# Loads of keys and queries around the block sums, transposes a batch ahead: a block-sparse attention with a gated feed-forward

## The chip, the cores and the metric

One core of a Trainium2 chip. The metric is the device time of one execution in microseconds (us), lower is better. A run counts as slow when it is over 1.5% above the fastest run of the same kernel; comparisons use fast runs only. With one core there is no second die to compare with, so this label rests on the time alone. In the profiles PE is TensorE's matmuls and PEld its weight loads, DVE is VectorE, ACT ScalarE, POOL GpSimd, and SP (its queue: SPq) SyncE. The granted clock is the TensorE clock that the throttle granted, 1.00 at full speed.

## The reference, cut to what matters

```python
# q, k, v: (4 batches, 8 heads, 768 positions, 64), float32
k_sum = k.reshape(B, H, 24, 32, D).max(axis=3)      # peak key of each block of 32
v_sum = v.reshape(B, H, 24, 32, D).mean(axis=3)     # mean value of each block
scores_l = scale * q @ k^T, only where |i - j| < 16
scores_s = scale * q @ k_sum^T + log(32)
a = softmax(concat([scores_l, scores_s]))
attn = a @ concat([v, v_sum])
x = attn.transpose(0, 2, 1, 3).reshape(3072, 512)
out = (sigmoid(x @ w_gate) * (x @ w_val)) @ w_out   # 512 -> 1536 -> 512
```

## The kernel before

The feed-forward network (FFN) of batch b is the base stream: 24 units of gate and value matmuls (`m1`, line L506) and 12 half-units of output matmuls for each half of the batch (`m2`). The attention steps of batch b+1 are dropped between these units by a slot number. So a step that waits holds up its engine, and with it the FFN behind it.

```python
def load_nat(b):                       # keys and queries of a batch, 16 casting DMAs
    ...
    for h in range(H):
        for nat, tap in ((kn, k), (qn, q)):
            nc.gpsimd.dma_start(out=nat[:, h // 2, :, ...], in_=tap[b, h]...)

def load_values(b):                    # one DMA for the whole batch
    load_v(b, 0, NU + 1) ...

# Attention steps
def D(self, p):                        # two transposing DMAs of a head pair, on SyncE's queue
    nc.sync.dma_start_transpose(kTn <- keys);  nc.sync.dma_start_transpose(qT <- queries)
def K(self, p): ...                    # DVE: peak keys (L254), then spread into kTx (L260, L262)
def L(self, g): ...                    # DMA: value rows by block, into vm
def R(self, g): ...                    # GpSimd: block sums of vm by halving additions (L417)
def M(self, g): ...                    # GpSimd: cast (L430), then a small DMA into vx
def B(self, g): ...                    # DVE: copies of the means inside vx (L435)
def H(self, g): ...                    # DVE: copies of neighbour rows inside vx, the halo (L365)
def A(self, p): ...                    # PE: probabilities times vx (L452), then DVE
def Y(self, p): ...                    # transposing DMA of the result into xT, on SyncE's queue
# T, Z, X: transposes and scores on PE; they play no part below

# end of the program's first part
load_values(1)
for g in range(2):
    a1.R(g)
...
NEXT = """
    3 T0   4 T1   5 Z0   6 T2   7 Z1   8 T3 M0 M1   10 Z2   12 Z3   13 H0 H1   15 B0 B1
    17 A0 A1   18 A2 A3 X0   19 X1   20 X2   21 X3"""
LATER = """
    0 R0 M0 R1 M1   2 K0   4 K1 D2   6 Z0 D3   8 K2 H0   10 Z1 H1   12 K3 B0   14 Z2 B1
    18 Z3   24 A0 A1   25 Y0   26 Y1   27 A2 A3   28 Y2   29 Y3"""
at[8].append(lambda: loads(2))
at.setdefault(14, []).append(lambda: block_rows(2))
at[23] = att[2].units("D0 D1")
```

GpSimd's queue is in order. It holds the casting loads and the block sums R, one behind the other, and this is where the change works.

The softmax here doesn't subtract the row's maximum and nothing guards it: scores larger than these inputs give would overflow.

Of the kernel before, what the change touches and what calls it, by code (L numbers as in the profile page):

```python
# [16 lines left out]
def kernel(  # L17
# [10 lines left out]
    nc = tc.nc  # L28

    B, H, S, D = q.shape  # L30
# [6 lines left out]
    NP = H // 2  # L37
    NU = H * NQ
# [21 lines left out]
    def ps(shape, dtype, name):  # L60
        return psum.tile(shape, dtype, name=name, tag="mm")

    def view(ap, off, dims):
        return bass.AP(ap.tensor, ap.offset + off, [list(ap.ap[0])] + [list(d) for d in dims])

    def rows_of(ap, off, dims):
        return bass.AP(ap.tensor, ap.offset + off, [list(d) for d in dims])
# [21 lines left out]
    def clear_ones(i):  # L89
        nc.vector.memset(vx_t[i][0:W, :, 64:66], 1.0)  # L90
        nc.vector.memset(vx_t[i][W:128, :, 64:66], 32.0)
# [29 lines left out]
    def make_zband():  # L121

        nc.vector.memset(zband, 0.0)
        with nc.allow_low_precision("zeros and ones"):
            nc.vector.tensor_reduce(out=zband[:, 29:32], in_=view(identp[0:W], 0, [[32, 3], [1, 32]]),
                                    axis=AX.X, op=ALU.add)
# [9 lines left out]
    def big():  # L136
        return vm_pool.tile([128, 2048], FP32, name="vm", tag="vm")

    def small():
        return nat_pool.tile([128, 3072], BF16, name="nat", tag="nat")  # L140

    def load_rows(tap, b, h0, nh, s0, n, st, queue=None):

        T = n // 128
        (queue or nc.gpsimd).dma_start(
            out=st.rearrange("p h t d -> p h (t d)"),
            in_=tap[b, h0:h0 + nh, s0:s0 + n, :].rearrange("h (p t) d -> p h (t d)", t=T))

    def load_nat(b):

        kn = small().rearrange("p (a c d) -> p a c d", a=NP, c=6)
        qn = small().rearrange("p (a c d) -> p a c d", a=NP, c=6)
        for h in range(H):
            for nat, tap in ((kn, k), (qn, q)):
                nc.gpsimd.dma_start(  # L155
                    out=nat[:, h // 2, :, 64 * (h % 2):64 * (h % 2) + 64],
                    in_=tap[b, h].rearrange("(c p) d -> p c d", p=128))
        return kn, qn

    def load_v(b, u0, u1, r0=0, r1=64):  # L160

        nc.gpsimd.dma_start(  # L162
            out=vx_t[b % 2][r0:r1, u0:u1, 0:64],
            in_=rows_of(v[b, 0, 0:1], (QT * u0 - 16 + r0) * D, [[D, r1 - r0], [QT * D, u1 - u0], [1, D]]))

    def load_values(b):
        if b + 1 < B:
            load_v(b, 0, NU + 1)
        else:
            load_v(b, 0, NU)  # L170
            load_v(b, NU, NU + 1, 0, 16)

    wg_bf = const.tile([128, NP, d_ff], BF16, name="wg")
# [365 lines left out]
    def run(base, at):  # L539
        for i, u in enumerate(base):  # L540
            u()
            for x in at.get(i, ()):
                x()

    def slots(text, a):
        at, slot = {}, None
        for w in text.split():
            if w.isdigit():
                slot = int(w)
            else:  # L550
                at.setdefault(slot, []).extend(a.units(w))
        return at
# [3 lines left out]
    att = [Attention(b, xTs[b]) for b in range(B)]  # L556


    a0 = att[0]

    k0 = [bf_pool.tile([128, 2, 6, 64], BF16, name="k0", tag="k0") for _ in range(NP)]
    qraw = small().bitcast(FP32).rearrange("p (h t d) -> p h t d", h=H, t=3)
    q0 = small().rearrange("p (a h t d) -> p a h t d", a=2, h=H, t=3)
    a0.ks = lambda p: k0[p]
    a0.qs = lambda p: q0[:, 0, 2 * p:2 * p + 2]
    a0.q2 = q0[:, 1]
    load_rows(q, 0, 0, 4, 0, HALF, qraw[:, 0:4], nc.sync)
    load_rows(q, 0, 4, 4, 0, HALF, qraw[:, 4:8], nc.sync)
    load_rows(k, 0, 0, 2, 0, S, k0[0])
    load_rows(k, 0, 2, 2, 0, S, k0[1])  # L570
    make_ident()
    load_rows(k, 0, 4, 2, 0, S, k0[2])
# [29 lines left out]
    load_wo(8, 4)  # L602

    nc.scalar.memzero(a0.heads(0, H, 0, 6, vx_t[0][96:128, 0:NU, 0:64]))
    f0 = Ffn(0, xTs[0])
    idle = ps([128, 512], FP32, "idle")
    a0.warm(idle[:, 0:128], 36)
    for i in range(2):
        clear_keys(i)
    make_masks()  # L610
# [1 line left out]
    for i in range(2, 4):  # L612
        clear_keys(i)
    a0.T1(0)
    a0.warm(idle[:, 0:128], 4)
    a0.T2(0, "dve")
    a0.S1(0, 0)
    a0.T1(1)
    a0.T2(1, "dve")
    a0.S1(0, 1)  # L620
    make_zband()
    a0.T1(2)
    a0.S1(1, 0, 4)
    a0.S1(1, 1)
    a0.T2(2, "dve")
    a0.T1(3)
    a0.S1(2, 0, 4)
    a0.S1(2, 1)
    a0.T2(3, "act")
    a0.S1(3, 0, 4)  # L630
    a0.halo(0, 2, 0, 6)
    a0.sums(0)
    a0.S1(3, 1)
    last = psum2.tile([128, 2, 512], FP32, name="last", tag="at")

    def wait(n):
        a0.warm(last[:, 0, 0:128], n)

    a0.means(0)
    a0.near(0)  # L640
    a0.halo(2, 4, 0, 6)
    a0.sums(1)
    a0.means(1)
    a0.far(0)
    a0.near(1)
    wait(4)
    a0.X(0, 0)
    a0.far(1)
    a0.halo(4, 6, 0, 6)
    a0.sums(2)  # L650
    a0.means(2)
    wait(4)
    a0.near(2)
    a0.X(1, 0)
    a0.far(2)
    a0.halo(6, 8, 0, 6)
    a0.sums(3)
    a0.means(3)
    wait(4)
    a0.near(3)  # L660
    a0.X(2, 0)
    f0.m1(0, 0, 0, 1)
    wait(4)
    a0.far(3)
    f0.m1(0, 0, 1, 2)
    wait(6)
    f0.m1(0, 0, 2, 3)
    wait(6)
    a0.X(3, 0)
    wait(10)  # L670
    a0.E(0)
    more_masks()
    f0.m1(0, 0, 3, 4)
    clear_ones(1)
    load_values(1)
    for g in range(2):
        a1.R(g)

    def loads(b):
        if b < B:  # L680
            att[b].nat = load_nat(b)
            load_values(b)

    def block_rows(b):
        if b < B:
            att[b].L(0)
            att[b].L(1)
# [5 lines left out]
        3 T0   4 T1   5 Z0   6 T2   7 Z1   8 T3 M0 M1   10 Z2   12 Z3   13 H0 H1   15 B0 B1  # L693
        17 A0 A1   18 A2 A3 X0   19 X1   20 X2   21 X3"""
    LATER = """
        0 R0 M0 R1 M1   2 K0   4 K1 D2   6 Z0 D3   8 K2 H0   10 Z1 H1   12 K3 B0   14 Z2 B1
        18 Z3   24 A0 A1   25 Y0   26 Y1   27 A2 A3   28 Y2   29 Y3"""

    at = slots(REST, a0)
    run(f0.units1(0, 1), at)  # L700
    at = slots(NEXT, a1)
    at[8].append(lambda: loads(2))
    at.setdefault(14, []).append(lambda: block_rows(2))
    at[23] = att[2].units("D0 D1")
    run(f0.units1(1) + f0.units2(), at)
    for b in range(1, B):
        ffn = Ffn(b, xTs[b])
        at = {}
        if b + 1 < B:
            at = slots(LATER, att[b + 1])  # L710
            at.setdefault(1, []).append(lambda: loads(b + 2))
            at.setdefault(22, []).append(lambda: block_rows(b + 2))
            if b + 2 < B:
                at[32] = att[b + 2].units("D0 D1")
        run(ffn.units1(0) + ffn.units1(1) + ffn.units2(), at)


# [28 lines left out]
```

## Time and profile before

| | before |
|---|---|
| time, first three runs | 254.6, 254.91, 251.95 us |
| profiled run, span, mean granted clock | 251.89 us, 250.0 us, 0.993 |
| first FFN matmul of batch 1, of batch 2, of batch 3 | 89.74, 147.93, 199.20 us |
| length of the FFN stage of batch 1, of batch 2, and the rest | 58.2, 51.3, 50.8 us |

The starts in this table are those of each batch's first whole FFN matmul in PE's timeline; the lengths are their differences. I use them all through, because a change can then be read stage by stage. The page of the kernel before gives PE's busy tenths and the granted clock in 40 slices of 6.25 us each:

```profile
PE   6999996999998995999999999999999999999993
PEclk9999999999999999799999999999999999999999
```

The only slice of the clock below 9 is the seventeenth, which begins at 100 us. PE's lowest slice but for the last one, a 5, stands just before it. That is the wait in the FFN of batch 1 that the prediction starts from.

### The profile page before, as it was taken

How to read it: one execution, taken by the hardware profiler on the slowest of the kernel's cores; microseconds unless marked ns; L12 is line 12 of the kernel's file. 1: busy time of each engine (PE TensorE's matmuls, PEld its weight loads, DVE VectorE, ACT ScalarE, POOL GpSimd, SP SyncE). 2: the span in 40 equal slices, each digit the busy share in tenths (PEclk: the TensorE clock that was granted, in tenths of full speed). 3: DMA queues.
4: the chain of work that ended last, by engine and by line, in shares of the span. 5: the costliest groups of instructions: out<-in, count | busy, mean ns of one | idle time of the engine just before them, and what ended most of it. 6: DMA issues, size and time to landing. Idle time of an engine off the chain costs nothing.

```text
span 250.0 us, 5523 instructions
## 1 busy us (share of the span) xinstructions
PE 235.0 (94%) x2270; PEld 135.9 (54%) x2270; DVE 137.3 (55%) x270; ACT 108.9 (44%) x191; POOL 95.8 (38%) x117
## 2 busy tenths in 40 slices
PE   6999996999998995999999999999999999999993
PEld 6677553566644652455555455555655466565441
DVE  6865658649979313699763307798543034444000
ACT  4742586559841542354541123555511243333121
POOL 8977433199995799970683000000000000000000
PEclk9999999999999999799999999999999999999999
DMA  7999999999999999999999965700016310000132
GB/s 176 166 159 196 204 204 226 224 181 106 104 139 225 191 195 161 173 152 183 135 93 115 181 164 156 67 0 3 0 38 182 122 42 0 0 3 0 56 115 84
DMA packets 87265, 30.74 MB, mean 123 GB/s; under 512 B 73864, under 2 KB 83592, under 8 KB 86664
## 3 DMA queue, kind: packets, MB, share of 16 engines
q0 software_dynamic: 62448, 15.36, 90.1%
q1 hardware_dynamic: 24792, 15.02, 27.5%
q8 instruction: 18, 0.29, 0.6%
q14 instruction: 7, 0.06, 0.1%
HBM read 33.08 MB, written 6.29 MB: 158 GB/s over the span
## 4 chain that ended last, share of the span: by engine, by line
PE 76%; DVE 12%; DMA 5%; issue 4%; ACT 2%; DVEq 0%; ACTq 0%; POOLq 0%
PE m L523 22%; PE gp L506 21%; PE vp L506 20%; DMA kTn<-nat 3%; DVE hT L514 3%; PE sc L318 2%; PE av L452 2%; DMA k<-in_k_dram 2%; DVE vx L435 2%; DVE P L325 2%; DVE vx L365 2%; DVE kTx L254 2%; PE tp L207 2%; PE vsp L345 1%; PE br L479 1%
## 5 line engine op out<-in xcount | busy, mean ns | idle before, releaser
L514 DVE SCALAR_TENSOR_TENSOR hT<-gate,vp 128x384 bf16<-128x384 f32 x96 | 51.8, 551 | 66.3 <-PE vp L506 62.7
L506 PE MATMUL vp<-xT,wv 128*128 128x384 bf16 x384 | 79.7, 329 | 3.5 <-DVE hT L514 3.5
L506 PE MATMUL gp<-xT,wg 128*128 128x384 bf16 x384 | 79.8, 329 | 1.5 <-DVE hT L514 1.2
L513 ACT ACTIVATE gate<-gp 128x384 f32<-128x384 f32 x96 | 47.4, 493 | 57.7 <-DVE hT L514 32.4
L523 PE MATMUL m<-wo,hT 128*128 128x512 bf16 x288 | 64.5, 379 | 0.0
L506 PEld LDWEIGHTS <-wv 128*128 128x128 bf16 x384 | 37.8, 99 | 29.1 <-issue 4.9
L506 PEld LDWEIGHTS <-wg 128*128 128x128 bf16 x384 | 35.8, 98 | 25.9 <-issue 3.5
L523 PEld LDWEIGHTS <-hT 128*128 128x128 bf16 x288 | 27.5, 98 | 31.5
L417 POOL TENSOR_TENSOR vm<-vm 96x512 f32<-96x512 f32 (+3 forms) x36 | 33.0, 923 | 23.6 <-DMA vm<-in_v_dram 21.7
L528 ACT ACTIVATE ot<-m 128x512 f32<-128x512 f32 x24 | 14.3, 597 | 49.0 <-PE m L523 48.9
L324 ACT ACTIVATE P<-sc 128x768 bf16<-128x768 f32 x28 | 21.4, 812 | 6.7 <-PE sc L318 6.7
L325 DVE TENSOR_TENSOR P<-P,mask 128x768 bf16<-128x768 bf16 x28 | 15.9, 588 | 5.1 <-ACT P L324 4.2
L254 DVE TENSOR_REDUCE kTx<-kTn 128x24 bf16<-128x768 bf16 x16 | 15.0, 945 | 5.7 <-DMA kTn<-nat 4.4
L155 POOL DMA_DIRECT2D nat<-in_q_dram x16 | 14.6, 910 | 0.1
L155 POOL DMA_DIRECT2D nat<-in_k_dram x16 | 14.4, 899 | 0.3 <-PE gp L506 0.3
L461 DVE TENSOR_TENSOR xs<-av,rec 128x768 bf16<-128x768 f32 (+1 forms) x16 | 13.7, 857 | 0.7 <-DVE rec L459 0.2
L365 DVE COPY vx<-vx 32x792 bf16<-32x792 bf16 (+1 forms) x14 | 13.4, 961 | 0.4
L162 POOL DMA_DIRECT2D vx<-in_v_dram x9 | 12.2, 1369 | 2.2 <-DVE kTx L254 1.2
L482 ACT COPY xT<-br 128x384 bf16<-128x384 bf16 (+1 forms) x12 | 6.9, 585 | 12.7 <-PE br L479 12.7
L318 PEld LDWEIGHTS <-kTx 64*128 64x128 bf16 x336 | 5.9, 95 | 5.4 <-issue 5.1
L452 PEld LDWEIGHTS <-P 120*64 120x64 bf16 x336 | 6.1, 111 | 4.9 <-issue 3.1
L452 PE MATMUL av<-vx,P 120*64 120x65 bf16 x336 | 7.2, 197 | 1.2 <-DVE xs L461 1.2
(78 smaller groups left out, 148.3 us busy)
## 6 DMA issues: line engine op xcount, KB each, us to landing
out_dram<-ot SPq DMA_DIRECT2D x24, 256.0 KB, 2.2
vm<-in_v_dram SPq DMA_DIRECT2D x4, 768.0 KB
vx<-in_v_dram POOLq DMA_DIRECT2D x2, 776.0 KB, 24.2
wo<-in_moe_w_out_dram POOLq DMA_DIRECT2D x3, 512.0 KB, 20.5
vm<-in_v_dram POOLq DMA_DIRECT2D x2, 768.0 KB, 19.2
nat<-in_k_dram POOLq DMA_DIRECT2D x16, 96.0 KB, 5.3
nat<-in_q_dram POOLq DMA_DIRECT2D x16, 96.0 KB, 5.7
nat<-in_q_dram POOLq DMA_DIRECT2D x3, 384.0 KB, 14.0
```

The source lines that it names most:

```text
L155: nc.gpsimd.dma_start(out=nat[:, h // 2, :, 64 * (h % 2):64 * (h % 2) + 64], in_=tap[b, h].rearrange("(c p) d -> p c d", p=128))
L254: nc.vector.tensor_reduce(out=self.kTx[p][:, t, W:KX], in_=self.kTn[p][:, 16:16 + S].rearrange("p (n w) -> p n w", w=32), axis=AX.X, op=AL ...
L324: nc.scalar.activation(out=Ph, in_=sc[:, :, 0:6 * QT], func=ACT.Exp, scale=SCALE)
L325: nc.vector.tensor_tensor(out=Ph, in0=Ph, in1=mask[:, None, 6 * hf:6 * hf + 6, :].rearrange("p i t w -> p i (t w)") .to_broadcast([128, 2, ...
L365: nc.vector.tensor_copy(out=self.heads(h0, h1, t0, t1, self.vx[64:96, 0:NU]), in_=self.heads(h0, h1, t0, t1, self.vx[0:32, 1:NU + 1]))
L417: nc.gpsimd.tensor_tensor(out=st[:, o:o + m], in0=st[:, o:o + m], in1=st[:, n + o:n + o + m], op=ALU.add)
L452: nc.tensor.matmul(out=av[r:r + 64, t // 6, (t % 6) // 2, i, 0:65], lhsT=P[0:KX, i, t, :], rhs=vx[0:KX, NQ * (2 * p + i) + t, 0:65], start ...
L506: nc.tensor.matmul(out=o, lhsT=wb[:, c, 128 * f:128 * (f + 1)], rhs=self.xT[:, c, HALF * hf:HALF * (hf + 1)], start=(c == 0), stop=(c == N ...
L513: nc.scalar.activation(out=gate, in_=gp, func=ACT.Tanh, scale=0.5)
L514: nc.vector.scalar_tensor_tensor(out=self.hT[hf][:, f, :], in0=gate, scalar=1.0, in1=vp, op0=ALU.add, op1=ALU.mult)
L523: nc.tensor.matmul(out=self.m3, lhsT=self.hT[hf][:, f, 128 * tt:128 * (tt + 1)], rhs=wo_bf[:, f], start=(f == 0), stop=(f == NF - 1))
L528: nc.scalar.mul(out=ot, in_=self.m3, mul=0.5)
```

## The change

The intent: the transposes of a batch should have landed before its FFN neighbour begins, for which its keys and queries have to be loaded earlier. So half of batch 2's sixteen loads go in front of batch 1's block sums, where GpSimd idled 8.18 us, and the transposes move into the stage before. The values come in four DMAs, so that a step need not wait for the whole. At the start of the program the first keys come uncast on the second queue and are cast on ACT, and the first attention steps are ordered anew, with fewer warm-up matmuls.

```diff
-    def load_nat(b):
+    def load_nat(b, h0, h1):
 ...
     def load_values(b):
-        if b + 1 < B:
-            load_v(b, 0, NU + 1)
-        else:
-            load_v(b, 0, NU)
+        for p in range(NP):
+            load_v(b, 24 * p, 24 * p + 24 + (p == NP - 1 and b + 1 < B))
+        if b + 1 == B:
             load_v(b, NU, NU + 1, 0, 16)
 ...
+    load_rows(k, 0, 0, 2, 0, S, kraw, nc.sync)
     load_rows(q, 0, 0, 4, 0, HALF, qraw[:, 0:4], nc.sync)
     load_rows(q, 0, 4, 4, 0, HALF, qraw[:, 4:8], nc.sync)
-    load_rows(k, 0, 0, 2, 0, S, k0[0])
 ...                        # + one ACT copy k0[0] <- kraw, new order of the first steps
     load_values(1)
+    load_nat(2, 0, 4)
     for g in range(2):
         a1.R(g)
 ...
-        0 R0 M0 R1 M1   2 K0   4 K1 D2   6 Z0 D3   8 K2 H0   10 Z1 H1   12 K3 B0   14 Z2 B1
+        0 R0 M0 R1 M1   2 K0   4 K1   6 Z0   8 K2 H0   10 Z1 H1   12 K3 B0   14 Z2 B1
 ...
-    at[8].append(lambda: loads(2))
+    at[8] += [lambda: load_nat(2, 4, H), lambda: load_values(2)]
     at.setdefault(14, []).append(lambda: block_rows(2))
-    at[23] = att[2].units("D0 D1")
+    for i, s in enumerate((16, 18, 20, 22)):
+        at.setdefault(s, []).extend(att[2].units(f"D{i}"))
 ...                        # in the FFN of batch 1, for batch 3:
-                at[32] = att[b + 2].units("D0 D1")
+                for i, s in enumerate((25, 27, 29, 31)):
+                    at.setdefault(s, []).extend(att[b + 2].units(f"D{i}"))
```

More of the change, by code (lines that the diff above doesn't have):

```diff
@@ L147, in load_rows @@
             in_=tap[b, h0:h0 + nh, s0:s0 + n, :].rearrange("h (p t) d -> p h (t d)", t=T))
-    def load_nat(b):
-        kn = small().rearrange("p (a c d) -> p a c d", a=NP, c=6)
-        qn = small().rearrange("p (a c d) -> p a c d", a=NP, c=6)
-        for h in range(H):
-            for nat, tap in ((kn, k), (qn, q)):
+    def load_nat(b, h0, h1):
+        if h0 == 0:
+            att[b].nat = [small().rearrange("p (a c d) -> p a c d", a=NP, c=6) for _ in range(2)]
+        for h in range(h0, h1):
+            for nat, tap in zip(att[b].nat, (k, q)):
                 nc.gpsimd.dma_start(
@@ L157, in load_nat @@
                     in_=tap[b, h].rearrange("(c p) d -> p c d", p=128))
-        return kn, qn
     def load_v(b, u0, u1, r0=0, r1=64):
@@ L562 @@
     qraw = small().bitcast(FP32).rearrange("p (h t d) -> p h t d", h=H, t=3)
+    kraw = big()[:, 0:768].rearrange("p (h t d) -> p h t d", h=2, t=6)
     q0 = small().rearrange("p (a h t d) -> p a h t d", a=2, h=H, t=3)
@@ L604 @@
     nc.scalar.memzero(a0.heads(0, H, 0, 6, vx_t[0][96:128, 0:NU, 0:64]))
+    nc.scalar.copy(out=k0[0], in_=kraw)
     f0 = Ffn(0, xTs[0])
     idle = ps([128, 512], FP32, "idle")
-    a0.warm(idle[:, 0:128], 36)
+    a0.warm(idle[:, 0:128], 32)
     for i in range(2):
@@ L614 @@
     a0.T1(0)
-    a0.warm(idle[:, 0:128], 4)
+    a0.warm(idle[:, 0:128], 8)
     a0.T2(0, "dve")
@@ L620 @@
     a0.S1(0, 1)
-    make_zband()
-    a0.T1(2)
-    a0.S1(1, 0, 4)
-    a0.S1(1, 1)
-    a0.T2(2, "dve")
-    a0.T1(3)
-    a0.S1(2, 0, 4)
-    a0.S1(2, 1)
-    a0.T2(3, "act")
-    a0.S1(3, 0, 4)
+    a0.T1(2)
+    a0.T2(2, "dve")
+    a0.S1(1, 0, 2)
+    a0.S1(1, 1)
+    a0.T1(3)
+    a0.T2(3, "act")
+    a0.S1(2, 0, 2)
+    a0.S1(2, 1)
+    make_zband()
+    a0.S1(3, 0, 2)
     a0.halo(0, 2, 0, 6)
     a0.sums(0)
+    a0.means(0)
     a0.S1(3, 1)
@@ L637, in wait @@
         a0.warm(last[:, 0, 0:128], n)
-    a0.means(0)
     a0.near(0)
@@ L645 @@
     a0.near(1)
-    wait(4)
+    a0.halo(4, 6, 0, 6)
+    wait(2)
     a0.X(0, 0)
     a0.far(1)
-    a0.halo(4, 6, 0, 6)
     a0.sums(2)
     a0.means(2)
-    wait(4)
     a0.near(2)
+    a0.halo(6, 8, 0, 6)
     a0.X(1, 0)
     a0.far(2)
-    a0.halo(6, 8, 0, 6)
     a0.sums(3)
     a0.means(3)
-    wait(4)
     a0.near(3)
     a0.X(2, 0)
+    a0.far(3)
     f0.m1(0, 0, 0, 1)
     wait(4)
-    a0.far(3)
     f0.m1(0, 0, 1, 2)
-    wait(6)
+    wait(4)
+    a0.X(3, 0)
     f0.m1(0, 0, 2, 3)
-    wait(6)
-    a0.X(3, 0)
-    wait(10)
+    wait(8)
     a0.E(0)
@@ L680, in loads @@
         if b < B:
-            att[b].nat = load_nat(b)
+            load_nat(b, 0, H)
             load_values(b)
```

## The prediction

> **What bounds the kernel now.** I read the busy table first, then the chain of work that ended last in order of time, then a table of stretches, then the timelines of PE, DVE and GpSimd around each gap. TensorE is the bound: 235.0 of 250.0 us.
>
> ```profile
> PE 235.0 (94%) x2270; PEld 135.9 (54%) x2270; DVE 137.3 (55%) x270; ACT 108.9 (44%) x191; POOL 95.8 (38%) x117
> ```
>
> The FFN matmuls run back to back wherever nothing disturbs them (in the chain, four 384-wide matmuls take 0.65 us, six 512-wide 1.29 us). The last batch, which has no attention beside it, shows the floor: 199.4 to 246.1, 46.7 us, PE busy all the time. The FFN of batch 2, with batch 3's attention between, takes 148.1 to 199.4, 51.3 us. The FFN of batch 1 does the same kind of work but takes 89.9 to 148.1, 58.2 us. So 6.9 us are lost there. The FFN of batch 0 (25.3 to 89.9) also carries the second half of batch 0's attention, and batch 1's transposes on PE. The chain names the loss in batch 1:
>
> ```profile
> 89.91 0.65 PE gp L506 x4
> ...
> 91.13 7.43 DMA kTn<-nat
> ...
> 98.59 0.95 DVE kTx L254
> ...
> 100.56 1.28 PE vp L506 x4
> 101.84 1.28 PE gp L506 x4
> 103.12 1.22 PE vp L506 x4
> ...
> 104.80 0.76 PE gp L506 x4
> ```
>
> The first transposing DMA of batch 2 is issued at 91.13, as the stage begins, and lands 7.4 us later. The key peaks (L254) wait for it in DVE's order, with the FFN's own DVE step (L514) behind them, so PE runs out of PSUM: it idles 3.50 us and comes back at half speed (1.28 us where 0.65 is usual). The stretches, whose columns are busy time by engine, granted clock, DMA share and GB/s:
>
> ```profile
> 90.00:98.60 8.60, 7.05 (x44) 4.12 (x43) 1.67 (x4) 3.54 (x7) 7.96 (x11) 1.00 1.67 172
> 98.60:107.00 8.40, 6.44 (x50) 3.35 (x50) 6.18 (x13) 2.49 (x5) 8.40 (x11) 0.80 2.13 177
> 107.00:131.00 24.00, 22.77 (x199) 13.18 (x197) 20.08 (x33) 11.96 (x22) 13.15 (x14) 1.00 2.44 141
> ...
> 148.00:162.00 14.00, 14.00 (x109) 8.39 (x108) 9.55 (x19) 6.91 (x13) 0.00 (x0) 1.00 0.68 126
> ```
>
> The granted clock of 0.80 stands only in the stretch after the wait; from 107 on another 1.2 us is PE idle behind a crowded DVE.
>
> The other view that matters is GpSimd's timeline. It issues all casting loads, and it also adds up the value blocks (L417):
>
> ```profile
> 38.72 2.24 POOL L162 DMA_DIRECT2D vx<-in_v_dram  x1 [0.98 <-DMA nat<-in_q_dram]
> 49.15 11.78 POOL L417 TENSOR_TENSOR vm<-vm 96x512 f32<-96x512 f32 x12 [8.18 <-DMA vm<-in_v_dram]
> 60.88 0.74 POOL L430 CAST mb<-vm 96x64 bf16<-96x64 f32 x2
> 61.57 0.87 POOL L155 DMA_DIRECT2D nat<-in_k_dram  x1
> ```
>
> GpSimd idles 8.18 us, adds for 11.78 us, and only then issues batch 2's sixteen loads, to 75.7. The block means go on by a small DMA to the copies L435, which A0 needs. DVE reaches these at 75.33:
>
> ```profile
> 72.75 2.55 DVE vx L365 x2
> ...
> 75.33 3.64 DVE vx L435 x2
> ...
> 79.00 0.24 DVE rec L459
> ...
> 80.40 0.97 DVE xs L461
> ...
> 81.41 0.57 PE av L452 x24
> ```
>
> So today the means, cast by 61.6, have about 14 us in hand.
>
> **What the Trainium skill says.** "TensorE: Matmul & The Clock Gate", Part 1: The HAM clock gate: the clock falls to half after an idle window of about 3.4 us and returns after about as long a busy one. The trace agrees: 3.50 us of idling, then granted 0.50 from 101 to 103, and full clock at 105. "DMA: Bandwidth & Descriptors", Issuing engines are not separate DMA queues: a second queue shares the same 16 engines and saves only issue time. The trace agrees in part: the second queue moves its first 0.79 MB from about 2 to 5 us at up to 373 GB/s, and the software queue's first packets come at about 4.5, so who goes first does matter. The same page, Rules for kernel authors: a cast in a DMA must be issued from GpSimd; hence the uncast keys and a new copy on ACT. "SBUF — State Buffer", SBUF: two separate sides: DVE and GpSimd exclude each other on a shared port. The trace fits: the same L262 copy takes 0.23 us at 109.3 and 1.29 at 56.2, beside its additions.
>
> **The change part by part.**
>
> First keys. Now the DMA runs 1.25 to 6.22 and PE begins at 6.26. Uncast keys first on the second queue are 0.39 MB of a stream that moved that much by about 3.7; with completion I estimate 4.1, plus an ACT copy of 768 columns (0.80 us in the L212 rows) gives 5.0. The start gains about 1.2 us; q then lands 1 us later, and its cast has to follow the masks, so call it 0.8. The rest of the start drops 26 warm-up matmuls (90 to 64), all of them behind the first forty, at 0.06 to 0.1 us each, and moves score, halo and sum steps earlier. About 1 us. Together PE reaches the FFN of batch 0 about 2 us earlier.
>
> Transposes a batch ahead. For batch 2 they move from the last slot of batch 0's FFN and slots 4 and 6 of batch 1's to slots 16, 18, 20 and 22 of the stage before. The first must then be issued some 10 us before its consumer, against a landing of 7.4 to 8.9. The 3.50 us gap goes; the half clock goes (three groups of 0.63 excess, 1.9 us); some 0.3 of small waits around it. I take 5.7 of the 6.9 us, since the 1.2 of DVE crowding has another cause. For batch 3 they move too, but there nothing is waited for today (PE 14.00 of 14.00 after 148), so it gains nothing; its transposes now stand between those of xT in the second queue (1.25 us each), an estimated risk of 0 to 0.5 us.
>
> Loads around the block sums. This is where I expect the loss. The built order shows eight semaphores in turn for GpSimd's DMAs, so a load waits until the one eight before it has landed. Eight of batch 2's loads now stand ahead of the additions, and the last of these eight waits for the fourth value load. These additions don't need it. Today the value load lands 25.7 us after its issue at 38.72, so at 64.4 (its packets thin out from 62.5). The queue is full all this while, and splitting the load into four adds no bandwidth. So the additions begin at 63.5 to 65.3, not 49.15: 64.6, plus 11.8 of additions, plus 0.5 for the first cast gives 76.9; issue 0.9 and landing an estimated 1.7 gives 79.5. DVE's L435 copies start at 79.5, not 75.33. From them to the end of this FFN nothing shortens: today 75.33 to 89.91 is 14.6 us, so the stage ends at 94.1. PE will idle about 5 us before A0 and come back slow, but the DVE steps (to 86) hide that; I add nothing. The loss is 4.2 us, and it also swallows the 2 us of the start, because this chain hangs on the DMA queue, not on PE.
>
> Value loads in four. Issue costs more (2.89 us for three at the start against 2.24 for one big), 1.5 us of GpSimd a batch, off the path. The halo copies need only their heads, but they had no wait for values today.
>
> The later chain holds: batch 2's remaining loads are issued 77 to 84, its additions about 90 to 102, its means are needed about 114; its transposes leave at about 82 to 94.
>
> Sum: 250.0 + 4.2 - 5.7 = 248.5 us of span.
>
> **The rivals.** (1) The additions do not become late, because the value load lands earlier than I think or the copies have slack: then the start's 2 us and the transposes' 5.7 both count, and the span is about 242, 3% less. For it speak the 62.5 us at which packets thin out and 8.18 us of GpSimd idle time that just fit eight issues of 0.85; against it the wait chain above, which allows no addition before the fourth value load. (2) The delay is longer: additions slowed by DVE (6.41 us for six at 120.8 against 5.55 at 82.7), the means' DMA slow, the cold clock not hidden. Copies at 82 would end the stage at 97 and give 251. (3) The transposes land in time but DVE is the bound in batch 1's FFN (20.08 of 24 us busy from 107): then only 3.5 us come back, and the span is 250.5. The batch 2 FFN, with 12.55 us of DVE in 14 and PE at 13.86, speaks against it.
>
> **Range and chances.** The three runs before span 251.95 to 254.91, with a profiled run of 251.9 for a span of 250.0. 248.5/250.0 on the median of 254.6 gives 253.1; rival 1 gives 246.5, rival 2 about 255.5. Weighting rival 1 at three in ten I say 251.5, between 246.5 and 255.0. Faster by over 2% needs under 249.5, that is, copies L435 starting by about 76.5: 0.30. Slower needs a second delay: 0.03.
>
> **What would show it.** Right: no DMA wait at the head of batch 1's FFN, that stage near 52.5 us, clock 1.00 in it; L417's first addition at 63 to 66, its releaser or the issue before it a value load; L435 near 79.5 with DVE idle before it, PE idle before A0 about 4 to 6 us with a clock dip. PE's first transposes near 5.0. Wrong: additions before 60, or L435 still directly behind L365, in which case the kernel is about 3% faster; or a wait for kTn still at L254, in which case the early transposes were not early enough.

## The result, and the profile after

The changed kernel is right, and slower: a median of 263.24 us (261.87 to 264.65, four runs, all fast) against 253.27 us (251.49 to 254.91, four runs). The ratio is 1.0395, with a 95% interval of 1.0291 to 1.0500. Ratios here and below are the mean time of one kernel's fast runs over that of the other's in the same rounds, so not quite the ratio of the medians quoted. The profiled run of the changed kernel, with a span of 262.5 us, was the slowest of its four, and the profiled run before was a quick one, so the 12.5 us between the two profiles are some 2.5 more than the 10.0 between the medians.

Stage by stage, from PE's timelines:

| start of | before | after | added in the stage that ends there |
|---|---|---|---|
| FFN of batch 1 | 89.74 | 99.03 | +9.3 |
| FFN of batch 2 | 147.93 | 156.54 | -0.7 |
| FFN of batch 3 | 199.20 | 211.84 | +4.0 |
| end | 250.0 | 262.5 | -0.1 |

Line numbers after are one or two lower than before: L162 is now L161, L417 is L415, L435 is L433, L365 is L363, L452 is L450, L506 is L504. The page after:

```profile
PE 240.0 (91%) x2244; PEld 138.2 (53%) x2244; DVE 137.6 (52%) x270; ACT 109.6 (42%) x192; POOL 100.8 (38%) x125
...
PEclk9995999999996599997999997999999999999999
```

PE is busy 5 us more than before although it has 26 instructions fewer. The clock row goes with that: four dips instead of one, near 20, 84, 119 and 157 us, each with half-speed matmuls. They lead to the four places to look at.

The first is GpSimd's timeline: start, duration, instruction, and in brackets the idle time before it with what ended it.

```profile
46.97 1.02 POOL L161 DMA_DIRECT2D vx<-in_v_dram  x1 [2.21 <-DMA wo<-in_moe_w_out_dram]
...
67.14 0.82 POOL L155 DMA_DIRECT2D nat<-in_q_dram  x1 [0.65 <-DMA vx<-in_v_dram]
67.97 13.36 POOL L415 TENSOR_TENSOR vm<-vm 96x512 f32<-96x512 f32 x12
81.28 0.41 POOL L428 CAST mb<-vm 96x64 bf16<-96x64 f32 x2
...
95.75 0.95 POOL L161 DMA_DIRECT2D vx<-in_v_dram  x1 [4.95 <-DMA nat<-in_k_dram]
```

The additions start at 67.97 and have no wait of their own. The wait is that of the load before them, the eighth early one: it is issued when the fourth value load, issued at 46.97, has landed. Before, the additions began at 49.15. They also take 13.36 us rather than 11.78. The means therefore reach DVE and PE late (DVE's timeline, then PE's):

```profile
84.38 2.45 DVE L433 COPY vx<-vx 24x2904 bf16<-24x2904 bf16 x2 [7.22 <-DMA vx<-mb]
...
118.64 1.34 DVE L363 COPY vx<-vx 32x3168 bf16<-32x3168 bf16 x1 [3.18 <-DMA vx<-in_v_dram]
```

```profile
84.49 0.29 PE L450 MATMUL av<-vx,P 120*64 120x65 bf16 x2 [6.61 <-DMA vx<-mb]
...
120.62 0.81 PE L504 MATMUL gp<-xT,wg 128*128 128x384 bf16 x4 [3.21 <-DVE hT L512]
...
159.51 0.48 PE L504 MATMUL gp<-xT,wg 128*128 128x384 bf16 x1 [1.58 <-DMA xT<-xs]
```

These three PE lines stand at the three late dips of the clock. At 84 PE waited 6.61 us for the means. At 120 it waited 3.21 us for DVE, because the halo copy L363 stood in DVE's queue waiting for a value load. The chain that ended last names that load; it is the one that GpSimd issued at 95.75 after a wait of 4.95 us for yet another load:

```profile
95.75 22.77 DMA vx<-in_v_dram
```

At 159 PE waited for a transposed result of batch 2 (xT), which shares the second queue with batch 3's transposes. The table of stretches after, whose columns are length, busy time of PE, PEld, DVE, ACT and POOL with counts, granted clock, DMA share and GB/s:

```profile
66.00:84.50 18.50, 11.89 (x104) 5.78 (x104) 10.71 (x13) 6.61 (x11) 17.21 (x20) 0.90 0.53 34
84.50:99.00 14.50, 13.52 (x156) 7.83 (x157) 6.90 (x10) 4.17 (x6) 7.24 (x8) 0.78 1.29 180
...
117.00:126.00 9.00, 5.79 (x26) 2.95 (x25) 7.14 (x12) 2.00 (x5) 5.35 (x6) 0.81 1.74 192
156.50:164.00 7.50, 5.34 (x23) 2.54 (x22) 1.11 (x2) 1.58 (x3) 0.00 (x0) 0.77 0.75 192
```

The same stretches before, the first and the last of them:

```profile
66.00:84.50 18.50, 17.27 (x222) 9.27 (x221) 15.44 (x22) 7.60 (x13) 14.08 (x14) 1.00 1.50 176
...
156.50:164.00 7.50, 7.50 (x89) 4.46 (x87) 6.20 (x13) 4.59 (x9) 0.00 (x0) 1.00 0.60 56
```

In the first stretch before, the DMA engines moved 176 GB/s: batch 2's loads, issued from 61.57 on. After, they moved 34 GB/s: GpSimd is adding (17.21 of 18.50 us), and the loads behind the additions are not issued. That idle DMA time is missing later. This is the link between the first delay and the second one.

The fourth place is the start. The stretch from 20 to 25 us, before and after:

```profile
20.00:25.00 5.00, 4.97 (x92) 3.98 (x90) 2.51 (x9) 1.41 (x4) 3.29 (x5) 1.00 1.45 195
```

```profile
20.00:25.00 5.00, 5.00 (x63) 3.73 (x61) 2.74 (x9) 1.21 (x3) 2.78 (x4) 0.50 1.48 194
```

PE gets its first keys early, at 4.95 us rather than 6.26, but runs at half speed here. The last piece of the first group of FFN matmuls, after which they run in whole groups, starts at 26.81 rather than 25.34.

### The profile page after: what moved, and what is told of

It reads as the page before. It is cut to its first block, busy times and chain, and to the rows that moved or that the text cites. A ratio compares the mean times of both kernels' runs of the same rounds, so it can differ in the third digit from the quotient of the medians.

```text
span 262.5 us, 5499 instructions
## 1 busy us (share of the span) xinstructions
PE 240.0 (91%) x2244; PEld 138.2 (53%) x2244; DVE 137.6 (52%) x270; ACT 109.6 (42%) x192; POOL 100.8 (38%) x125
## 4 chain that ended last, share of the span: by engine, by line
PE 47%; DMA 35%; POOL 10%; DVE 3%; issue 2%; SPq 1%; ACT 0%; DVEq 0%; POOLq 0%; ACTq 0%
PE m L521 17%; DMA vx<-in_v_dram 16%; PE gp L504 14%; PE vp L504 14%; DMA wo<-in_moe_w_out_dram 6%; POOL vm L415 5%; DMA nat<-in_k_dram 5%; DMA wg<-in_moe_w_gate_dram 4%; DMA nat<-in_q_dram 3%; DVE hT L512 2%; PE av L450 1%; POOL wg L177 1%; POOL wv L177 1%; POOL vx L161 1%; DMA xT<-xs 1%
## 5 line engine op out<-in xcount | busy, mean ns | idle before, releaser
L504 PE MATMUL gp<-xT,wg 128*128 128x384 bf16 x384 | 81.7, 333 | 5.6 <-DVE hT L512 3.2
L504 PE MATMUL vp<-xT,wv 128*128 128x384 bf16 x384 | 80.7, 333 | 1.1 <-DVE hT L512 1.1
L521 PE MATMUL m<-wo,hT 128*128 128x512 bf16 x288 | 65.8, 385 | 0.0
L504 PEld LDWEIGHTS <-wv 128*128 128x128 bf16 x384 | 38.1, 99 | 29.1 <-issue 5.4
L504 PEld LDWEIGHTS <-wg 128*128 128x128 bf16 x384 | 36.3, 99 | 28.9 <-issue 6.6
L415 POOL TENSOR_TENSOR vm<-vm 96x512 f32<-96x512 f32 (+3 forms) x36 | 34.5, 969 | 1.9
L161 POOL DMA_DIRECT2D vx<-in_v_dram x18 | 16.9, 964 | 14.2 <-DMA nat<-in_k_dram 5.9
L323 DVE TENSOR_TENSOR P<-P,mask 128x768 bf16<-128x768 bf16 x28 | 18.7, 686 | 4.2 <-ACT P L322 3.2
L450 PE MATMUL av<-vx,P 120*64 120x65 bf16 x336 | 8.3, 209 | 7.6 <-DMA vx<-mb 6.6
L450 PEld LDWEIGHTS <-P 120*64 120x64 bf16 x336 | 7.2, 124 | 11.7 <-issue 10.8
L363 DVE COPY vx<-vx 32x792 bf16<-32x792 bf16 (+1 forms) x14 | 10.8, 779 | 3.6 <-DMA vx<-in_v_dram 3.2
L433 DVE COPY vx<-vx 24x2904 bf16<-24x2904 bf16 x6 | 6.1, 1025 | 7.3 <-DMA vx<-mb 7.2
```

The source lines that it names most:

```text
L161: nc.gpsimd.dma_start(out=vx_t[b % 2][r0:r1, u0:u1, 0:64], in_=rows_of(v[b, 0, 0:1], (QT * u0 - 16 + r0) * D, [[D, r1 - r0], [QT * D, u1 - ...
L323: nc.vector.tensor_tensor(out=Ph, in0=Ph, in1=mask[:, None, 6 * hf:6 * hf + 6, :].rearrange("p i t w -> p i (t w)") .to_broadcast([128, 2, ...
L415: nc.gpsimd.tensor_tensor(out=st[:, o:o + m], in0=st[:, o:o + m], in1=st[:, n + o:n + o + m], op=ALU.add)
L450: nc.tensor.matmul(out=av[r:r + 64, t // 6, (t % 6) // 2, i, 0:65], lhsT=P[0:KX, i, t, :], rhs=vx[0:KX, NQ * (2 * p + i) + t, 0:65], start ...
L504: nc.tensor.matmul(out=o, lhsT=wb[:, c, 128 * f:128 * (f + 1)], rhs=self.xT[:, c, HALF * hf:HALF * (hf + 1)], start=(c == 0), stop=(c == N ...
L521: nc.tensor.matmul(out=self.m3, lhsT=self.hT[hf][:, f, 128 * tt:128 * (tt + 1)], rhs=wo_bf[:, f], start=(f == 0), stop=(f == NF - 1))
```

## The experiments

Twelve kernels ran in three calls, each call on one chip beside runs of the kernel before on the same chip. All gave a correct result. In this table "additions" is the start and length of the block sums of batch 1, and FFN1 and FFN2 are the lengths of the stages of batches 1 and 2 in the profile; (s) marks a profile in the slow state, of which I use only what doesn't depend on the clock. The medians are of all runs, slow ones too. At a margin of 2% the recorded verdicts are slower for the change, unclear for early_only, early3, ahead2_only, no_front and xt_first, and same for the others; where I say slower or faster below, the interval leaves out 1.

| kernel | ratio of fast runs [95%] | median of all, us | additions | FFN1 | FFN2 |
|---|---|---|---|---|---|
| before (profile at hand) | 1 | 253.27 | 49.15, 11.78 | 58.2 | 51.3 |
| the change | 1.0395 [1.0291, 1.0500] | 263.24 | 67.97, 13.36 | 57.5 | 55.3 |
| early_only | 1.0322 [1.0222, 1.0422] | 261.07 | 67.08, 12.94 | 60.7 | 51.3 |
| early3 | 1.0125 [1.0030, 1.0220] | 255.73 | 56.87, 12.38 | 58.5 | 51.3 |
| loads_back | none | 255.32 | 53.92, 11.07 (s) | 52.3 (s) | 52.4 (s) |
| ahead2_only | 0.9865 [0.9772, 0.9958] | 250.29 | not used | 59.0 (s) | 51.3 (s) |
| no_front | 1.0318 [1.0216, 1.0419] | 259.94 | 65.69, 13.46 | 56.8 | 52.2 |
| front_only | 1.0048 [0.9976, 1.0121] | 256.53 | not used | not used | not used |
| xt_first | 1.0319 [1.0244, 1.0394] | 260.32 | not used | 57.3 | 51.3 |
| rows_later | 1.0057 [1.0015, 1.0098] | 255.31 | not used | 54.5 | 57.8 |
| good_parts | 0.9916 [0.9871, 0.9961] | 251.43 | 49.10, 11.18 | 54.7 | 53.6 |
| ahead2_v4 | 0.9866 [0.9811, 0.9921] | 249.23 | not used | 53.6 | 51.3 |
| kraw_only | 0.9960 [0.9918, 1.0003] | 253.87 | not used | not used | not used |
| v4_only | 1.0021 [0.9982, 1.0060] | 253.41 | not used | not used | not used |

One profile each gives the stage lengths. FFN2 is 51.3 us in every kernel that leaves that stage alone. FFN1 is not so steady: v4_only, kraw_only (s) and front_only (s), which leave it alone, have 60.0, 60.4 and 57.5 us where the kernel before has 58.2, so a difference of 1 or 2 us there is not resolved.

The theory: the early loads make the additions late, through the semaphores of GpSimd's DMAs. The built program uses eight of them in turn, so a load can be issued only after the one eight before it has landed. The trace of the changed kernel fits: the last six early loads waited for two pieces of the output weights and then the four value loads, each time the DMA eight places before. All else follows from the late additions. The rivals: the transposes that were moved cost more than they bring, or the new start does.

### early_only: the early loads alone

```diff
 # on the kernel before
     load_values(1)
+    load_nat(2, 0, 4)
     for g in range(2):
         a1.R(g)
 ...
-    at[8].append(lambda: loads(2))
+    at[8] += [lambda: load_nat(2, 4, H), lambda: load_values(2)]
```

> The kernel before with one thing alone: four heads (eight loads) of batch 2 issued ahead of the additions. Theory: the last of the eight waits for the value load, first addition at 65 to 67, mean copies at 80 to 84, batch 1's FFN starts 5 to 9 us late, the old kTn wait stays: span 255 to 259. Rival (only the issue time of eight loads, 6.8 us, counts, and it fits into the idle 8.2 us): first addition at 49 to 56, no change of time (250).

GpSimd's timeline, then DVE's:

```profile
66.25 0.82 POOL L155 DMA_DIRECT2D nat<-in_q_dram  x1 [5.52 <-DMA vx<-in_v_dram]
67.08 12.94 POOL L416 TENSOR_TENSOR vm<-vm 96x512 f32<-96x512 f32 x12
```

```profile
83.77 0.91 DVE L434 COPY vx<-vx 24x2904 bf16<-24x2904 bf16 x1 [2.90 <-DMA vx<-mb]
```

The last early load waits 5.52 us, for the value load, and then the additions run. The copies L434 start at 83.77, after a wait of 2.90 us for the means. PE itself waits only 2.22 us for them. Of the 7.1 us by which batch 1's FFN starts later (96.86), 4.3 were there when the output matmuls of batch 0 began (73.16 rather than 68.83), and 1.5 of these since the first FFN matmul (23.66 rather than 22.16). So a good part of the loss comes before the means are needed, as in early3 below. The kernel is 3.2% slower, which is most of the whole change, with the old transposes, the old start and the values in one DMA. The wait for kTn at the head of batch 1's FFN stays, at 6.30 us. So the early loads alone do not even bring what they were meant for.

### early3: one head fewer

```diff
 # early_only, but
-    load_nat(2, 0, 4)
+    load_nat(2, 0, 3)
```

> The same with three heads (six loads). Theory of the eight semaphores: the sixth load waits only for the second piece of the output weights, landed by 55.4 to 56, so the additions start at 56 to 58, the mean copies are ready before 75 and the time is that of the kernel before (249 to 251). Rival (any early load delays by its own cost or by loading the DMA engines, in proportion): three quarters of the loss that four heads bring.

If eight semaphores in turn are the cause, six early loads end their waits two DMAs before the value load. GpSimd's timeline:

```profile
56.87 12.38 POOL L416 TENSOR_TENSOR vm<-vm 96x512 f32<-96x512 f32 x12
```

The additions start at 56.87, in the range that the count gives, and 10 us earlier than with two loads more. Two loads take 1.6 us to issue, so it isn't the issuing. The time, though, was not that of the kernel before: 1.3% slower. The additions now fall beside more of batch 1's key steps on DVE. The spread copies of the keys in the stretch from 50 to 72 us, by shape (count, busy time, mean ns), in early3 and then in the kernel before:

```profile
L261 DVE COPY kTx<-kTx 128x264 bf16<-128x264 bf16 x4 | 5.8, 1450 | 0.0
```

```profile
L262 DVE COPY kTx<-kTx 128x264 bf16<-128x264 bf16 x4 | 3.2, 803 | 0.0
```

The same four copies take 2.6 us longer, and PE's output matmuls of batch 0 begin at 72.11 rather than 68.83; of these 3.3 us 1.2 were there at the first FFN matmul (23.34 rather than 22.16). This part of the expectation missed: a delay of the additions inside their 14 us of slack still costs time. That it does so by what they then run beside fits these lines; no run separates it.

### loads_back: the whole change, with all sixteen loads behind the additions

```diff
 # on the kernel after
-    load_nat(2, 0, 4)
-    at[8] += [lambda: load_nat(2, 4, H), lambda: load_values(2)]
+    at[8] += [lambda: load_nat(2, 0, H), lambda: load_values(2)]
```

> The changed kernel with all sixteen key and query loads of batch 2 issued behind the block additions again. Theory (the additions were late because the eighth early load waits for the fourth value load, and the later waits follow from that): first addition at 50 to 53 us instead of 67.97, the mean copies L433 at 75 to 77 instead of 84.4, batch 1's FFN starts at 90 to 91.5 instead of 99.0 and has no halo wait; the xT wait at the start of batch 2's FFN stays (4 us), so the span is about 249, 5% less than the changed kernel. Rival (the front, which ran cold, or the transposes ahead cost the time): span stays above 257.

Three of its four runs count as slow (255.29, 255.34, 255.91 us against 250.35), so there is no ratio, and the profile is a slow one with a half clock from 10 to 30 us. All four are below the changed kernel's fastest, 261.87, though on another chip. What doesn't depend on the slow start: the additions start at 53.92 and take 11.07 us, the head of batch 1's FFN waits neither for kTn nor for the halo, and that stage takes 52.3 us. Two expectations missed: the copies L433 came at 84.32, not 75 to 77, and batch 1's FFN began at 97.79, not 90 to 91.5, because the start, with a wait of 2.30 us for keys and then the half clock, had put the first FFN matmul at 31.45 (23.50 in the changed kernel). So such a cold start alone can put this stage as late as the early loads do. In this late stage the first transpose of keys landed 13.4 us after its issue; in good_parts below, on time, it takes 18.4. The wait for xT, which I expected to stay, shrank from 2.15 us to 0.91.

### no_front: the whole change, with the old start

```diff
 # on the kernel after
-    load_rows(k, 0, 0, 2, 0, S, kraw, nc.sync)
+    load_rows(k, 0, 0, 2, 0, S, k0[0])
-    nc.scalar.copy(out=k0[0], in_=kraw)
 ...                        # and the order and warm-ups of the kernel before
```

> The changed kernel with the old start. Theory (the block sums' chain hangs on the DMA queue, so the start matters little beyond its cold clock): additions still at 66 to 68, mean copies at 82 to 85, batch 1's FFN starts at 97 to 99, time 0 to 1.5% under the changed kernel: 259 to 263. Rival (the cold start is the main loss): 254 or less.

GpSimd's timeline:

```profile
65.69 13.46 POOL L415 TENSOR_TENSOR vm<-vm 96x512 f32<-96x512 f32 x12
```

It is still 3.2% slower. The additions start 2.3 us earlier than with the new start and the copies L433 at 82.13 rather than 84.38. The waits for the halo (2.32 us) and for xT (0.79) are there, smaller. So the loss doesn't need the new start. It does add to the delay through GpSimd's queue: with the first keys ahead of them on the second queue the first queries land later, their cast on GpSimd waits 2.40 us, and every load behind it is about 1.2 us late.

### good_parts: the change without early loads and with the old start

```diff
 # no_front, but
-    load_nat(2, 0, 4)
-    at[8] += [lambda: load_nat(2, 4, H), lambda: load_values(2)]
+    at[8] += [lambda: load_nat(2, 0, H), lambda: load_values(2)]
```

> The changed kernel without its two bad parts: old start, and all sixteen loads behind the additions; value loads in four and both batches' transposes ahead stay. Theory: additions at 50 to 53, batch 1's FFN starts at 90 to 92 and takes 52.5 to 55 us, batch 2's 51.3 to 53, span 245 to 248, 1 to 3% under the kernel before and 5 to 6% under the changed one. Rival (the transposes ahead are themselves slow in a crowded DMA, as in ahead2_only): 247 to 250, 0 to 1.5% under before.

GpSimd's timeline, then DVE's and PE's:

```profile
49.10 11.18 POOL L415 TENSOR_TENSOR vm<-vm 96x512 f32<-96x512 f32 x12 [2.59 <-DMA vm<-in_v_dram]
```

```profile
101.73 0.95 DVE L252 TENSOR_REDUCE kTx<-kTn 128x24 bf16<-128x768 bf16 x1 [2.58 <-DMA kTn<-nat]
```

```profile
148.05 0.32 PE L504 MATMUL gp<-xT,wg 128*128 128x384 bf16 x1 [1.63 <-DMA xT<-xs]
```

The additions are back at 49.10, waiting only for their own rows. The kernel is 0.8% faster than before. It differs from no_front by the early loads alone, and each was measured against the kernel before on its own chip: 1.0318 over 0.9916 is 1.0405, with an interval of some 1% to either side; the medians of all runs, each against its own, give 3.3%. The early loads cost 3 to 4%. With early_only, which has them alone, that settles the cause. With batch 1's FFN on time (from 90.56) a wait for kTn stays, 2.58 us at the second head pair, and the stage takes 54.7 us. And PE waits 0.31 and 1.63 us for xT, though nothing is late here.

### xt_first: batch 3's transposes back in their old slots

```diff
 # on the kernel after, for batch 3 only
-    for i, s in enumerate((25, 27, 29, 31)):
-        at.setdefault(s, []).extend(att[b + 2].units(f"D{i}"))
+    at[32] = att[b + 2].units("D0 D1")      # D2 and D3 in slots 4 and 6 of the next stage
```

> The changed kernel with batch 3's transposes back in their old slots, so that nothing stands between the xT transposes on the second queue. Theory: the waits for xT at the head of batch 2's FFN (0.57 and 1.58 us) and the half clock behind them go, that stage takes 51.3 to 52 instead of 55.3 us, time 1 to 1.7% under the changed kernel: 258.5 to 261. Rival (the xT wait came from elsewhere, as from late batch 1): stage unchanged at 55, time unchanged.

The stretch in which the changed kernel waited for xT, taken from the same point of the stage:

```profile
155.90:163.40 7.50, 7.50 (x48) 4.52 (x47) 4.21 (x9) 3.19 (x7) 0.00 (x0) 1.00 0.56 154
```

PE is busy throughout at full clock, and the stage of batch 2 is back at 51.3 us. So the 4.0 us lost there come from batch 3's transposes standing between the transposes of xT in the second queue. The first and the last transpose of xT on SyncE's queue, before and in the changed kernel:

```profile
135.27 2.60 SPq L470 DMA_TRANSPOSE xT<-xs  x2
...
141.74 1.25 SPq L470 DMA_TRANSPOSE xT<-xs  x1
```

```profile
143.87 1.41 SPq L468 DMA_TRANSPOSE xT<-xs  x1
...
156.94 1.26 SPq L468 DMA_TRANSPOSE xT<-xs  x1
```

From the first to the last it was 6.5 us and is now 13.1, with four transposes of batch 3 between. Lateness isn't needed: in good_parts it is 12.9 us, with waits of 1.94 us together and 2.3 us lost (53.6 against 51.3), while no_front, which is late, waits 0.79 us and loses 0.9. The changed kernel waited 2.15 us, about as long as good_parts; what it lost beyond that goes with its half clock (0.50 from 160 to 162 us), which good_parts didn't have (1.00 from 145 to 154).

The whole time is less clear. The interval overlaps that of the changed kernel, and in this profile the start ran at half clock from 10 to 30 us. The additions start at 69.46 here, but PE reaches the matmuls that need the means at 87.24, after the copies (85.19), and waits for neither: a cold start can hide the delay of the means.

### ahead2_only: batch 2's transposes ahead, and nothing else

```diff
 # on the kernel before
-    at[23] = att[2].units("D0 D1")
+    for i, s in enumerate((16, 18, 20, 22)):
+        at.setdefault(s, []).extend(att[2].units(f"D{i}"))
 ...                        # and no D2, D3 in batch 1's FFN
```

> The kernel before with batch 2's transposes alone moved to slots 16, 18, 20 and 22 of the stage before. Theory: the kTn wait and the half clock at the head of batch 1's FFN go, that FFN takes 52 to 54 us instead of 58.2, span 244 to 246, 2% faster. Rival (the transposes, issued ahead of the output stores on one queue, wait for the late loads and block what stands behind them, or stretch the loads): little gain or none, 249 to 252.

The times of its three fast runs are 1.35% better than before. Its profile, a slow run, shows why it isn't more. SyncE's queue, then DVE:

```profile
77.52 2.33 SPq L223 DMA_TRANSPOSE kTn<-nat  x1
80.03 7.19 SPq L223 DMA_TRANSPOSE qT<-nat  x1
```

```profile
95.49 0.95 DVE L253 TENSOR_REDUCE kTx<-kTn 128x24 bf16<-128x768 bf16 x1 [0.57 <-DMA kTn<-nat]
...
103.11 0.95 DVE L253 TENSOR_REDUCE kTx<-kTn 128x24 bf16<-128x768 bf16 x1 [4.60 <-DMA kTn<-nat]
```

The first transpose is issued 13.6 us earlier than before (77.52 rather than 91.13), but lands only about 3 us earlier, at 95.5 rather than 98.5: it is under way for 18 us among the loads. The issue of the next one alone takes 7.19 us. The wait of 4.12 us for the first pair became one of 4.60 for the second. I expected the stage at 52 to 54 us; in this profile it took 59.0, so where the fast runs gain their 1.35% is not shown. Issuing it 13.6 us earlier brought the landing forward by only 3.

### rows_later: the block rows moved instead

```diff
 # ahead2_only, and batch 2's block rows loaded after its transposes
-    at.setdefault(14, []).append(lambda: block_rows(2))
+    at[22].append(lambda: block_rows(2))
 ...                        # B0 and B1 moved from slots 12 and 14 to 17 and 20
```

> ahead2_only, with batch 2's block rows (two loads of 768 KB) issued behind the four transposes instead of ahead of them, and the mean copies later in batch 1's FFN. Theory (in ahead2_only the transposes were issued at 77.5 but landed at 95.5, because loads and stores filled the engines, 18 us instead of 7.4): they now land before 92, the wait for kTn at the head of batch 1's FFN goes, that FFN takes 52 to 54 us; span 243.5 to 246, 2 to 3% under the kernel before. Rival (the transposes are slow by themselves on that queue, or the block sums are then late): wait for kTn stays, or a new wait for the means, no gain over ahead2_only (247 to 249).

This leaves the transposes less company. The wait for kTn went and the stage of batch 1 took 54.5 us. But the sums of batch 2 came late now, and with them batch 3's loads. GpSimd's timeline, then PE's:

```profile
103.61 7.32 POOL L416 TENSOR_TENSOR vm<-vm 96x512 f32<-96x512 f32 x6 [24.07 <-DMA vm<-in_v_dram]
```

```profile
147.44 0.32 PE L505 MATMUL gp<-xT,wg 128*128 128x384 bf16 x1 [2.73 <-DMA xT<-xs]
```

The stage of batch 2 took 57.8 us, and the whole was 0.6% slower than before. The delay moved on by a batch.

### front_only and kraw_only: the new start

```diff
 # front_only, on the kernel before: the uncast first keys, the new order, fewer warm-ups
+    load_rows(k, 0, 0, 2, 0, S, kraw, nc.sync)
-    load_rows(k, 0, 0, 2, 0, S, k0[0])
+    nc.scalar.copy(out=k0[0], in_=kraw)
-    a0.warm(idle[:, 0:128], 36)
+    a0.warm(idle[:, 0:128], 32)
 ...
 # kraw_only: the first three lines alone
```

> The kernel before with the new start alone (uncast first keys, the new order and the fewer warm-up matmuls). Theory from the profiles of the changed kernel and of loads_back (clock 0.89 over the first 30 us, cold from 9 to 33 us in loads_back): the first transposes at 5.0 instead of 6.26, but the second keys come later (PE idle 1 to 2.3 us there), the clock falls to half in the first 30 us in most runs, the first whole FFN group starts at 26 to 33 us instead of 25.3, time 0 to 2% above before, mean clock 0.95 to 0.985. Rival (the start gains the predicted 2 us): first whole group at 23.5 to 24.5, time 0 to 1% under before.

> The kernel before with the uncast first keys on the second queue alone, in the old order with all the old warm-up matmuls. Theory A (the first keys push the second keys, and PE's idle time there makes the clock fall): clock at half in some stretch of the first 30 us in the profile, mean clock under 0.98 in most runs. Theory B (the 26 warm-up matmuls that were taken out kept the clock up): clock 1.00 through the start, first whole FFN group at 24 to 25.3, time as before or 0.3% less.

Neither differs from the kernel before in fast runs by more than the interval allows. Of 20 runs of front_only 13 had a mean clock below 0.98, and 11 of 40 of the kernel before in the same call; of kraw_only's 20 it was six, and 15 of 59 of the kernel before. Front_only's median was 256.53 us against 254.29, and its profile, a slow run, shows PE busy 5.00 of 5 us from 10 to 15 at a clock of 0.50. Kraw_only's profile, slow too, has the clock below 0.9 in two slices between 6 and 19 us, so its theory B (full clock at the start) doesn't hold there; nor does A, which wanted a mean clock under 0.98 in most runs. So the new start may make the state with a low clock more frequent. But that is a difference between slow runs, and I draw nothing from it: what the start is worth stays open, between -0.2% and +1.2%.

### v4_only: values in four DMAs

```diff
 # on the kernel before
     def load_values(b):
-        if b + 1 < B:
-            load_v(b, 0, NU + 1)
+        for p in range(NP):
+            load_v(b, 24 * p, 24 * p + 24 + (p == NP - 1 and b + 1 < B))
 ...
```

> The kernel before with the value loads in four DMAs alone. Theory: 1.5 us more of GpSimd a batch, off the path: time within 0.7% of before. Rival (the split alone delays the additions or the batch 2 loads): 1% or more slower.

No difference: 1.0021, and the interval holds 1.

### ahead2_v4: what is left when each losing part is taken out

```diff
 # good_parts, with batch 3's transposes in their old slots as in xt_first
```

> The same with only batch 2's transposes ahead. If batch 3's bring nothing (nothing waited for them before), the same time as good_parts within 0.5%; if they cost something by standing between the xT transposes, up to 1% faster than good_parts.

All six runs are fast, 248.43 to 250.24 us. It beats both kernels: 1.3% under the kernel before. The stage of batch 1 takes 53.6 us and that of batch 2 51.3, and its page has a full clock in every slice. Against good_parts the gain is 0.5%, with overlapping intervals, and ahead2_only, without the values in four, has the same ratio; so what is measured is that batch 2's transposes ahead are worth some 1.3% (0.8 to 1.9% by this interval), not which of these three is best. A wait for kTn of 0.71 us is left at the second head pair.

## Why the prediction was wrong

The prediction named the right loss by the right mechanism, and missed its size and where else it would come out. Its sum was +4.2 in the stage before batch 1's FFN, -5.7 in batch 1's FFN, 0 to 0.5 in batch 2's. It came out as +9.3, -0.7 and +4.0. I had given a slower kernel 3 in 100, because it "needs a second delay"; two came.

- **The additions become late: right, too small.** Predicted at 64.6, they started at 67.97. Without the new start they started at 65.69, so 2.3 of the 3.4 us go with the new start, which delays GpSimd's queue. I had written that the start's gain would be swallowed; it was a loss in this queue. In early_only the single value load landed near 66.2 rather than the 64.4 I had read off the trace before. It was issued at 40.23 rather than 38.72 and took 26.0 us rather than 25.7, so the early loads beside it hardly slowed it.
- **The additions' length: wrong.** I took 11.78 us from the old place. They took 13.36, and 12.94 and 13.46 in early_only and no_front, against 11.07 and 11.18 in loads_back and good_parts, where they were early. I had the slower rate at hand in rival 2 and didn't put it into the sum.
- **From the additions' end to the copies: right.** 3.1 us predicted, 3.05 measured (81.33 to 84.38). So the copies were 4.9 us later than predicted (84.38 for 79.5): 3.4 from the additions' later start and 1.6 from their length.
- **From the copies to the end of the stage: right in the sum, by luck.** 14.6 us predicted, 14.65 measured. Inside it the copies took 2.45 us rather than 3.64, and the half clock after PE's 6.61 us of idling gave that back: six 512-wide matmuls took 2.74 us. I had said DVE would hide it. Two errors cancelled.
- **The gain in batch 1's FFN: the step that failed most.** The wait for kTn at L254 did go, but not because the transposes landed in the 7.4 to 8.9 us that I had taken: the first landed 14.7 us after its issue at 86.46, in a stage that itself began 9.3 us late. In good_parts, whose stage is on time, it took 18.4 us, and a wait of 2.58 us stayed at the second pair. And "the later chain holds" was wrong. Because the additions held up GpSimd, the loads behind them were issued late, again each waited for the one eight before, and a piece of batch 2's values was issued at 95.75 and landed at 118.5. I had the eight loads issued from 77 to 84 (they were, from 81.63 to 88.85) and had not applied the rule of eight to the value pieces behind them. The halo copy needed that piece at about 115, so a new wait with a new half clock took the place of the old one. The gain was 0.7 us instead of 5.7. With the loads behind the additions the halo wait is gone, and the stage took 54.7 us in good_parts; the 52.3 of loads_back, near my 52.5, came with a stage that began 7 us later in the profile. My step on the halo said that it had no wait for values "today"; I did not ask what would become of it when the loads are late.
- **Batch 3's transposes: wrong size.** I had 0 to 0.5 us for their standing between those of xT. I had counted single transposes of 1.25 us. Four of them stood before the last transpose of xT, which left 13.1 us after the first rather than 6.5. It cost 4.0: two waits (0.57 and 1.58 us) and the half clock at and after them. xt_first brings it all back.
- **The start: first step right, the rest wrong.** PE's first transposes came at 4.95, predicted 5.0. The second keys were not there then (PE idles 0.75 us at 7.84), and from 19 to 26 us the clock was at half. A gain of 2 us at the FFN of batch 0 became a loss of 1.5 in this profile. Its share in the time of fast runs is not resolved.

The transposes a batch ahead were the good part, if smaller than I thought: batch 2's save about 1.3% of the time, about 3 us, in ahead2_only and ahead2_v4. Rival 2 (a longer delay) was the direction in which it went, but it ended at 251 us of span, because none of my three rivals let the delay of one batch's sums pass on to the loads of the next.

## What to carry to other kernels

A load that is moved ahead of compute on an in-order engine brings its own waits with it: before moving it, count which earlier DMA its completion semaphore belongs to, and take that landing as the earliest start of all that stands behind it. Then follow the delay once around the loop, since a queue that is late for one batch issues the next batch's loads late, too. And issuing a transfer earlier into full DMA engines doesn't make it land earlier by the same time; look where it lands.

## What the Trainium skill lacked or had wrong

- "DMA: Bandwidth & Descriptors", Rules for kernel authors, advises to issue a DMA early, compute, and wait for it late. It doesn't say what an early issue costs when completion semaphores are few and used in turn, so that the issue itself waits: here eight early loads alone moved the additions behind them from 49.15 to 67.08 us (early_only), six of them only to 56.87 (early3), and the early loads cost 3 to 4% of the time.
- The same page, Latency and other measured facts, has a bandwidth of 261 GB/s for the DMA transpose with a non-contiguous middle dimension, from which 128 by 768 bf16 elements (197 KB) are an estimated 0.75 us. It has nothing on a transpose beside a queue of many small loads: here one landed 18 us after its issue (77.52 to 95.5), and 7.4 us after it in the kernel before, and the issue of one held SyncE's queue for 7.19 us.
- "TensorE: Matmul & The Clock Gate", Part 1: The HAM clock gate, has an idle window of about 3.4 us before the clock halves. Of the changed kernel's four dips the one after 6.61 us of idling fits that, and the one after 3.21 us about fits. The one at 159 us followed two waits of 0.57 and 1.58 us, 2.15 together, and the one from 19 to 26 us came with PE busy 5.00 of 5 us and no wait longer than 0.75 us since 5 us. In good_parts 0.31 and 1.63 us, 1.94 together, set off none. No run here settles what set these two off.
- "SBUF — State Buffer" has no figure for additions on GpSimd beside copies on DVE, by operation and shape: here the twelve additions took 11.07 to 13.46 us, longer where they were late, and four DVE copies 3.2 or 5.8 us.
